# Storing a normalised activation in DRAM with the reloaded three quarters of each channel first

## The chip, the cores and the metric

The kernel runs on one core of a Trainium2 chip. The metric is the device time of one execution in microseconds (us), lower is better. The kernel before takes 1568.49 us (median; 1566.84 to 1569.18).

The engines are called PE (matmul), PEld (its weight loads), DVE (vector), ACT (activations), POOL (GpSimd) and SP or SyncE. SyncE computes nothing here; it issues DMAs. A "q" after an engine's name in the profile (SPq) means its instruction queue. L32 is the line of a helper through which most operations are recorded, so tiles, not lines, tell the operations apart. To "issue" a DMA is to start it by an instruction; it "lands" when its data has arrived, which it tells on a semaphore, a counter that other instructions can wait for. A packet is what a DMA engine moves at a time, in these traces one contiguous run.

## The reference, cut to what matters

An image of 512 x 512 pixels and 96 channels goes through a depthwise 3x3 convolution, a layer norm over the channels, a 96-to-384 matmul with gelu, a global response norm, a 384-to-96 matmul, and a residual add.

```python
h = _layernorm(out, axis=-1)                  # out: the depthwise convolution
h = jnp.einsum('bhwc,ce->bhwe', h, w1)        # C = 96 -> 4C = 384
h = _gelu(h)
gx = jnp.sqrt((h * h).sum(axis=(1, 2), keepdims=True) + 1e-6)   # over the whole image
nx = gx / (gx.mean(axis=-1, keepdims=True) + 1e-6)
h = grn_gamma * (h * nx) + grn_beta + h
h = jnp.einsum('bhwe,ec->bhwc', h, w2)
return x + h
```

The norm `gx` needs a sum over the whole image before any output can be made. So the kernel has two phases: phase 1 computes the gelus once and sums their squares, phase 2 makes the output. The gelus of the whole image are 201 MB (262,144 pixels x 384 x 2 B); the kernel keeps a quarter of them in DRAM and computes the rest a second time.

## The kernel before

The image is cut into 128 blocks of 4 rows (`GR = 4`, `W = 512`). `yn` is the layer norm's result for a block. In phase 1 POOL writes `yn` to SBUF with the row and a third of the channels on the partitions, and SyncE turns it into channels on partitions by way of DRAM: four writes, one for each row, then one read. One quarter of each row's gelus (the "kept" quarter) is also stored in DRAM. Phase 2 reloads `yn`, expands the other three quarters again, and loads the kept one. The last two blocks (`is_res`) stay on chip.

```python
def yn_rows(q):                       # phase 2's load: three quarters of each row
    k = kept_quads(q) * 128           # 128, or 256 for the last two blocks
    return yn_dram[q:q + 2].rearrange("q c (r w) -> (q c) r w", r=GR)[0:128, :, k:]

def yn_dst(q, r):                     # phase 1's write of row r
    return yn_dram[q].rearrange("(c i) (r w) -> r c i w", i=NI, r=GR)[r]
# ...
def stage_write(b):
    yn = yns.pop(b)                   # [128 = 4 rows x 32, NI = 3, W = 512]
    for r in range(GR):
        sp.dma_start(out=yn_dst(b, r), in_=yn[32 * r:32 * r + 32, :, :])

def stage_read(b):
    t = yn_ring[b % NYT]
    sp.dma_start(out=t[:C], in_=yn_src(b))
```

In a slot of phase 1 SyncE's instructions stand in this order; it works them off one by one, and waits in that order too:

```python
load_x(s + 4)                         # input, 432 KB
stage_read(...)                       # yn back: waits until that block's writes have landed
stage_write(...)                      # four writes
stage_bcast(...); stage_rows(...)     # 4 and 2 small DMAs, each once in four blocks
store()                               # kept gelus (g_dram), 384 KB, waits for ACT
```

Phase 2, two parts:

```python
(pq if q % 3 == 0 else sq).dma_start(                # kept gelus: every third load from POOL
    out=kept[:].rearrange("p t j w -> p (t j w)"), in_=g_dram[q])
# ...
LEAD = RES * UPB + 2                                 # 8 gelu units ahead at the start
even = LEAD + (n * NSUB + sub + 1) * (total + 2 - LEAD) / (NSUB * NBLK)   # 2 at the end
```

Of the kernel before, what the change touches and what calls it, by code (L numbers as in the profile page):

```python
# [12 lines left out]
GR = 4  # L13
# [40 lines left out]
def kernel(  # L54
# [13 lines left out]
    bf16 = x.dtype  # L68
    assert bf16 == mybir.dt.bfloat16

    B, H, W, C = x.shape
# [3 lines left out]
    NI = C // 32  # L75
# [6 lines left out]
    NQ = GR * W // QW  # L82
    dram = ctx.enter_context(tc.tile_pool(name="dram", bufs=1, space=bass.MemoryType.DRAM))
    g_dram = dram.tile([NBLK, 128, NCH * QW], bf16, name="g_dram")
    yn_dram = dram.tile([NBLK, C, GR * W], bf16, name="yn_dram")
    r_dram = dram.tile([NBLK, GR, W], bf16, name="r_dram")

    def is_res(q):
        return q >= NBLK - RES

    def cm_quads(q):
        return 3 if q % 3 and not is_res(q) else 2

    def kept_quads(q):
        return 2 if is_res(q) else 1
# [4 lines left out]
    PXP = GR * W // 128  # L100
    MB = W // PXP

    def quad(flat_ap, t):
        return flat_ap.rearrange("p r (t g m) -> p t g r m", t=NQ, m=MB)[:, t]

    def quad_out(flat_ap):
        return flat_ap.rearrange("p (g r m) -> p g r m", r=GR, m=MB)

    def yn_src(q):
        return yn_dram[q].rearrange("c (r w) -> c r w", r=GR)  # L110

    def yn_rows(q):
        k = kept_quads(q) * 128
        return yn_dram[q:q + 2].rearrange("q c (r w) -> (q c) r w", r=GR)[0:128, :, k:]

    def yn_dst(q, r):
        return yn_dram[q].rearrange("(c i) (r w) -> r c i w", i=NI, r=GR)[r]

    consts = ctx.enter_context(tc.tile_pool(name="consts", bufs=1))
    prepool = ctx.enter_context(tc.tile_pool(name="pre", bufs=1))  # L120
# [8 lines left out]
    w1p = consts.tile([128, E], bf16, name="w1p")  # L129
# [14 lines left out]
    grp = {}  # L144
    res_g = {q: prepool.tile([128, 2, NCH, QW], bf16, name=f"resg{q}") for q in range(NBLK - RES, NBLK)}
    NYT = 6
    yn_ring = [prepool.tile([128, GR, W], bf16, name=f"ynT{i}") for i in range(NYT)]

    ynts = {}

# [9 lines left out]
    with ExitStack() as p1:  # L160
        pe, dve, act, pool, sp = (InOrder(tc, e) for e in (nc.tensor, nc.vector, nc.scalar, nc.gpsimd, nc.sync))
# [32 lines left out]
        zrow = consts.tile([128, W], bf16, name="zrow")  # L194
# [15 lines left out]
        make_identity(nc, ident_f[:])  # L210
        pool.memset(Wq[:], 0.0)
        for t in yn_ring:
            pool.dma_start(out=t[C:128, :, :], in_=zrow[C:128, None, :].to_broadcast([128 - C, GR, W]))
        dve.tensor_copy(out=ident_b[:], in_=ident_f[:])
        for q in range(GR):
            dve.tensor_copy(out=eye32[32 * q:32 * q + 32, :], in_=ident_f[32 * q:32 * q + 32, 32 * q:32 * q + 32])
# [12 lines left out]
        for i in range(NXT):  # L229
            t = xtpool.tile([128, NI, SL * MB], bf16, name=f"xT{i}")  # L230
# [6 lines left out]
        def stage_load(n, sq, pq):  # L237
            q = ORDER[n]
            v = (ORDER[0] + n) % NYT
            r0 = q * GR  # L240
            if is_res(q):
                kept, ynt = res_g[q], ynts[q]
            else:
                kept = late.gl.tile([128, 1, NCH, QW], bf16, name="gl")
                (pq if q % 3 == 0 else sq).dma_start(  # L245
                    out=kept[:].rearrange("p t j w -> p (t j w)"), in_=g_dram[q])
                ynt = yn_ring[v]
                sq.dma_start(out=ynt[:, :, kept_quads(q) * 128:], in_=yn_rows(q))
            xr = late.xr.tile([128, PXP, C], bf16, name="xr")
            pq.dma_start(out=xr[:], in_=x[0, r0:r0 + GR].rearrange("r w c -> (r w) c").rearrange(  # L250
                "(p g) c -> p g c", g=PXP))
            grp[q] = dict(kept=kept, ynt=ynt, xr=xr)

        def recompute_units(q):
            nk = kept_quads(q)
            ynt = grp[q]["ynt"]

            def fresh(j):
                if j == 0:
                    grp[q]["made"] = late.gr.tile([128, NCH, (NQ - 1) * QW], bf16, name="gr")  # L260
                if is_res(q):
                    U = psU.tile([128, 2, QW], f32, name="U")
                else:
                    U = late.psU2.tile([128, NQ - 1, QW], f32, name="U2")
                for t in range(nk, NQ):
                    pe.matmul(quad_out(U[:, t - nk, :]), lhsT=w1p[:, j * 128:(j + 1) * 128],
                               rhs=quad(ynt[:], t), start=True, stop=True)
                n = (NQ - nk) * QW
                act.activation(out=grp[q]["made"][:, j, :n], in_=U[:].rearrange("p k w -> p (k w)")[:, :n],
                                func=ACTF.Gelu_apprx_tanh)  # L270

            return [lambda j=j: fresh(j) for j in range(NCH)]
# [73 lines left out]
        for i in range(NI):  # L346
            dve.tensor_copy(out=dwx[:, i], in_=dw9[:, None, chans(i)].to_broadcast([9, GR, 32]))
            pe.matmul(Ud[:, i, :], lhsT=dwx[:, i].rearrange("p q c -> p (q c)"), rhs=ident_b[:9, :9],
                      start=True, stop=True)
# [3 lines left out]
        n = 0  # L353
        for h in range(2):
            for j in range(GR):
                for q in (2 * h, 2 * h + 1):
                    a = q + GR * shift(h, j) - j + 1
                    if 0 <= a < 3:
                        n += 1
                        (dve if n % 2 else pool).tensor_copy(out=Wq[32 * q:32 * q + 32, :, :, j, :],  # L360
                                        in_=Wd[32 * q:32 * q + 32, :, 3 * a:3 * a + 3, :])
# [227 lines left out]
        def stage_write(b):  # L589
            yn = yns.pop(b)  # L590
            for r in range(GR):
                sp.dma_start(out=yn_dst(b, r), in_=yn[32 * r:32 * r + 32, :, :])

        def stage_read(b):
            t = yn_ring[b % NYT]
            sp.dma_start(out=t[:C], in_=yn_src(b))
            ynts[b] = t

        bsts = {}
# [8 lines left out]
        def px0(b):  # L608
            return NCH * QW * (cm_quads(b) - 2)

        def mlp_units(b):
            gsh = res_g[b] if is_res(b) else gshpool.tile([128, 2, NCH, QW], bf16, name="gsh")
            gms[b] = gmpool.tile([128, TAIL], bf16, name="gm")
            yt = ynts[b]

            def cm_mm(dst, j, t):
                pe.matmul(quad_out(dst), lhsT=w1p[:, j * 128:(j + 1) * 128], rhs=quad(yt[:], t), start=True, stop=True)

            def pair(j):
                U = psU.tile([128, 2, QW], f32, name="U")  # L620
                for t in range(2):
                    cm_mm(U[:, t, :], j, t)
                act.activation(out=gsh[:, :, j, :], in_=U[:], func=ACTF.Gelu_apprx_tanh)

            def rest(n):
                U = psU.tile([128, 2, QW], f32, name="U")
                Uf = U[:].rearrange("p k w -> p (k w)")
                c0 = 2 * QW * n
                c, end = c0, c0 + 2 * QW
                while c < end:  # L630
                    if c < px0(b):
                        j, sz = c // QW, QW
                        cm_mm(Uf[:, c - c0:c - c0 + sz], j, 2)
                    else:
                        k, e0 = divmod(c - px0(b), E)
                        sz = min(E - e0, 512 - c % 512, end - c)
                        t, r = divmod(k, GR)
                        col = (cm_quads(b) + t) * 128
                        pe.matmul(Uf[:, c - c0:c - c0 + sz], lhsT=yt[:, r, col:col + 128], rhs=w1p[:, e0:e0 + sz],
                                  start=True, stop=True)  # L640
                    c += sz
                act.activation(out=gms[b][:, c0:end], in_=Uf, func=ACTF.Gelu_apprx_tanh)

            def entry(j, m, src):
                k, e = divmod(ents[b] + m, 32)
                if k not in bsts:
                    bsts[k] = bstpool.tile([128, NCH, 32, 6], f32, name="bst")
                dve.bn_stats(out=bsts[k][:, j, e, :], in_=src)

            def squares(j):  # L650
                for m in range(2):
                    entry(j, m, gsh[:, m, j, :])

            def squares_rest():
                if px0(b):
                    for j in range(NCH):
                        entry(j, 2, gms[b][:, j * QW:(j + 1) * QW])

            def store():
                sp.dma_start(out=g_dram[b], in_=gsh[:, 0].rearrange("p j w -> p (j w)"))  # L660

            return pair, rest, squares, squares_rest, store

        def gram_mms(b):
# [22 lines left out]
        for k, (b0, n) in enumerate(BATCHES):  # L687
# [16 lines left out]
            for b in range(b0, b0 + n):  # L704
# [4 lines left out]
                m = s + (3 if ramp else 4)  # L709
# [11 lines left out]
        for s in range(last_slot + 1):  # L721
# [3 lines left out]
            for b in get("read"):  # L725
                stage_read(b)
            for b in get("write"):
                stage_write(b)
# [49 lines left out]
            else:  # L778
                b = mlp[0]
# [51 lines left out]
            for n in {2: (0, 1, 2), 1: (3, 4)}.get(last_slot - s, ()):  # L831
                stage_load(n, sp, pool)
# [14 lines left out]
    with p2:  # L847
# [14 lines left out]
        r = gi[:].bitcast(f32)  # L862
        for it in range(3):
# [5 lines left out]
            r = rn_[:]  # L869
# [28 lines left out]
        for n, q in enumerate(ORDER):  # L898
            if n + PRE < NBLK:
                stage_load(n + PRE, nc.sync, nc.gpsimd)  # L900
            if n + 2 < NBLK:
                stage_xb(ORDER[n + 2], nc.gpsimd, B2c)
            if n == NBLK - 1:
                stage_out(*held)
                held = None
            o_sb = stage_mm2(n, q)
            if held:
                stage_out(*held)
            held = (q, o_sb)
# [30 lines left out]
```

## Time and profile before

| stretch | length | what fills it |
|---|---|---|
| phase 1, to the first gelu of phase 2 | 1021.0 us | PE and ACT 94% in the middle; SyncE 71% (below) |
| phase 2, from there to the end | 542.2 us | ACT 99%, PE 99%, POOL 94%, DMA share 1.03 (1120 to 1500 us) |

The windows view gives each engine's busy us in a stretch, with the number of instructions, then the granted PE clock, the mean busy share of the 16 DMA engines (packet times summed over 16 engines' time, so it can read a little over 1), and GB/s. The kernel before, the middle of phase 1 and most of phase 2:

```profile
core 0: us, PE busy (x) PEld busy (x) DVE busy (x) ACT busy (x) POOL busy (x), PEclk, DMA share, GB/s
...
400.00:700.00 300.00, 281.96 (x5117) 141.58 (x5114) 257.12 (x438) 281.12 (x280) 267.19 (x201) 1.00 0.77 237
```

```profile
1120.00:1500.00 380.00, 376.52 (x5304) 274.24 (x5303) 201.22 (x374) 375.85 (x277) 356.79 (x218) 1.00 1.03 387
```

No column shows SyncE: issuing a DMA is not counted as busy. It has to be read from the timeline of its queue. Two blocks of the kernel before (start in us, duration in us, instruction, how many merged):

```profile
607.30 0.33 SPq L32 DMA_DIRECT2D ynT<-yn_dram  x1
607.68 2.56 SPq L32 DMA_DIRECT2D yn_dram<-yn  x4
610.28 2.21 SPq L32 DMA_DIRECT2D rbc<-r_dram  x4
612.61 0.55 SPq L32 DMA_DIRECT2D g_dram<-gsh  x1
613.26 0.37 SPq L32 DMA_DIRECT2D xin<-in_x_dram  x1
614.39 0.33 SPq L32 DMA_DIRECT2D ynT<-yn_dram  x1
614.76 2.53 SPq L32 DMA_DIRECT2D yn_dram<-yn  x4
618.00 0.33 SPq L32 DMA_DIRECT2D g_dram<-gsh  x1
618.75 0.34 SPq L32 DMA_DIRECT2D xin<-in_x_dram  x1
622.61 0.33 SPq L32 DMA_DIRECT2D ynT<-yn_dram  x1
```

The four writes of `yn` are the largest item: about 0.6 us each. They are issue times alone; the semaphore records show that such a write lands 4.5 us after its issue (median, 400 to 700 us). The Trainium skill, "Perfetto Trace Analysis", DMA Instruction — HWDGE, says the same of the recorded window: it runs from the semaphores being satisfied until the sequencer is free, and the data movement is not in it. Gaps such as 614.39 less 613.63 (when the load of x was issued) are waits. Who ended them, in the same 300 us (total us, times, longest):

```profile
SPq L32 <- DMA yn_dram<-yn: 42.0, 32, 4.7
SPq L32 <- POOL yn L32: 18.2, 10, 4.0
SPq L32 <- DVE rt L32: 10.8, 7, 1.9
SPq L32 <- DVE xT L32: 8.0, 12, 2.5
```

In this text, SyncE's *occupied* time is the sum of the durations of its instructions plus the step from one to the next (about 45 ns; up to 55 ns of each gap is counted so); the rest of its gaps is *wait*. Over 100 blocks (block 20 to 120, from the start of one block's first gelu to the next one's) the kernel before takes 7.41 us a block, of which SyncE is occupied 5.29 us (issues 4.73, steps 0.57) and waits 2.11 us.

### The profile page before, as it was taken

To read this page: it belongs to the slowest core of one execution; us is meant where nothing else is said; L and a number is where in the kernel's file an instruction comes from. 1 tells how busy PE (TensorE), PEld (TensorE's weight loads), DVE (VectorE), ACT (ScalarE), POOL (GpSimd) and SP (SyncE) were. 2 spreads that over 40 slices of the span, in tenths; PEclk is the share of its full clock that TensorE was granted. 3 is DMA by queue.
4 is the path that set the end of the run, shared out by engine and by line. 5 is a ranking of instruction groups with operands and counts; after the bars stand their busy time and mean duration, and the time that the engine had idled before them with its cause. 6 is when DMAs were issued, how large, how long until landed. Compare 5 with 4: busy or idle time off the path is not lost. (4 is left out here: it accounts for less than half of the span.)

```text
span 1563.2 us, 55720 instructions
## 1 busy us (share of the span) xinstructions
PE 1450.2 (93%) x23749; PEld 844.8 (54%) x23749; DVE 1129.5 (72%) x2027; ACT 1447.1 (93%) x1306; POOL 1314.2 (84%) x933
## 2 busy tenths in 40 slices
PE   7888999999999999999999997789999999999997
PEld 3444444444444444444444444457777777777765
DVE  6748978888898888889888888855555555555544
ACT  3889989999999999999999999989999999999997
POOL 3559888998989898998889897459999999999994
PEclk9999999999999999999999999999999999999999
DMA  5668787787778677777778667869999999999993
GB/s 148 182 182 269 224 262 217 240 254 227 225 234 259 210 249 244 230 235 237 247 210 243 213 197 230 268 238 387 393 379 396 387 397 388 383 381 388 379 372 147
DMA packets 235470, 427.94 MB, mean 274 GB/s; under 512 B 34102, under 2 KB 148374, under 8 KB 235222
## 3 DMA queue, kind: packets, MB, share of 16 engines
q1 hardware_dynamic: 219972, 356.59, 70.2%
q0 software_dynamic: 13888, 67.64, 11.4%
q8 instruction: 186, 3.05, 0.8%
q14 instruction: 62, 0.51, 0.1%
q10 hardware_dynamic: 1362, 0.15, 0.1%
HBM read 272.78 MB, written 150.72 MB: 271 GB/s over the span
## 5 line engine op out<-in xcount | busy, mean ns | idle before, releaser
L32 PE MATMUL U<-ynT,w1p 128*128 128x512 bf16 x2166 | 603.1, 380 | 43.5 <-ACT gm L32 8.7
L32 DVE BATCH_NORM_STATS2 bst<-gsh 128x6 f32<-128x512 bf16 x756 | 468.7, 673 | 128.9 <-ACT gsh L32 128.4
L32 ACT ACTIVATE gr<-U 128x1536 bf16<-128x1536 f32 (+1 forms) x384 | 521.0, 1450 | 17.3 <-PE U L32 14.6
L32 POOL TENSOR_TENSOR yn<-y_bf,rbc 128x1536 bf16<-128x1536 bf16 x128 | 396.9, 3103 | 81.0 <-ACT rbc L32 29.7
L32 DVE TENSOR_TENSOR o_sb<-O,xb 128x384 bf16<-128x384 f32 x512 | 277.5, 557 | 252.2 <-PE O L32 179.7
L278 POOL TENSOR_TENSOR xb<-xr,B2c 128x1536 f32<-128x1536 bf16 x126 | 394.9, 3134 | 43.4 <-DVE B2c L32 35.2
L32 ACT ACTIVATE gsh<-U 128x1024 bf16<-128x1024 f32 x378 | 369.4, 1024 | 55.8 <-ACT gm L32 29.6
L32 ACT ACTIVATE gm<-U 128x1024 bf16<-128x1024 f32 x384 | 368.1, 1035 | 0.6 <-PE U L32 0.5
L32 PE MATMUL Y<-xT,Wq 64*32 64x511 bf16 (+1 forms) x8694 | 320.9, 388 | 9.8 <-DVE B2bc_f L32 3.7
L32 POOL TENSOR_TENSOR ysq<-y_bf 128x1536 bf16<-128x1536 bf16 x114 | 313.2, 2748 | 14.0 <-ACT y_bf L32 13.4
L32 PEld LDWEIGHTS <-w1p 128*128 128x128 bf16 x2166 | 169.4, 97 | 277.9 <-issue 174.2
L32 PEld LDWEIGHTS <-gr 128*128 128x128 bf16 x4584 | 228.7, 98 | 84.4 <-ACT gr L32 12.1
L32 PE MATMUL O<-W2s,gr 128*128 128x96 bf16 x4584 | 251.3, 206 | 12.1 <-ACT gr L32 9.4
L32 PEld LDWEIGHTS <-Wq 64*32 64x32 bf16 x9216 | 102.2, 90 | 187.5 <-issue 146.9
L32 PE MATMUL U<-w1p,ynT 128*128 128x384 bf16 (+2 forms) x1032 | 161.3, 272 | 33.7 <-ACT gm L32 30.6
L32 ACT ACTIVATE y_bf<-Y 128x1536 bf16<-128x1536 f32 x121 | 175.1, 1447 | 16.6 <-PE Y L32 16.4
L32 DVE STREAM_TRANSPOSE xT<-xin 128x576 f32<-128x576 f32 (+1 forms) x256 | 181.2, 747 | 3.2 <-DMA xin<-in_x_dram 3.1
L32 DVE BATCH_NORM_STATS2 bst<-gm 128x6 f32<-128x512 bf16 x252 | 156.5, 676 | 0.9 <-ACT gm L32 0.9
L32 PEld LDWEIGHTS <-ynT 128*128 128x128 bf16 x1032 | 88.7, 96 | 90.8 <-issue 69.4
L32 PE MATMUL SG<-gm 128*128 128x128 bf16 x2064 | 136.3, 219 | 0.5 <-ACT gm L32 0.3
L32 PEld LDWEIGHTS <-gm 128*128 128x128 bf16 x2064 | 121.0, 98 | 11.5 <-issue 0.5
L250 POOL DMA_DIRECT2D xr<-in_x_dram x123 | 67.6, 549 | 27.6 <-POOL xb L278 27.6
(103 smaller groups left out, 700.3 us busy)
## 6 DMA issues: line engine op xcount, KB each, us to landing
ynT<-yn_dram SPq DMA_DIRECT2D x254, 384.0 KB
xin<-in_x_dram SPq DMA_DIRECT2D x126, 432.0 KB
yn_dram<-yn SPq DMA_DIRECT2D x512, 96.0 KB
xr<-in_x_dram POOLq DMA_DIRECT2D x128, 384.0 KB, 6.6
out_dram<-o_sb SPq DMA_DIRECT2D x127, 384.0 KB
g_dram<-gsh SPq DMA_DIRECT2D x126, 384.0 KB
gl<-g_dram SPq DMA_DIRECT2D x84, 384.0 KB
gl<-g_dram POOLq DMA_DIRECT2D x42, 384.0 KB, 6.4
```

The costliest lines, as they stand in the source:

```text
L32: r = f(*a, **k)
L250: pq.dma_start(out=xr[:], in_=x[0, r0:r0 + GR].rearrange("r w c -> (r w) c").rearrange("(p g) c -> p g c", g=PXP))
L278: pq.tensor_tensor(out=xb[:], in0=grp[q]["xr"][:], in1=bias[:, None, :].to_broadcast([128, PXP, C]), op=ALU.add)
```

## The change

Intent: phase 2 loads the three quarters it expands as four runs of 768 B for each channel. If those quarters lie together in DRAM, it is one run of 3 KB, a quarter of the packets. The SBUF tile gets the same order. For this, each row's write in phase 1 has to be split in two, for the two regions. Core of the diff:

```diff
     def yn_rows(q):
+        n = GR * (NQ - kept_quads(q)) * 128
+        return yn_dram[q:q + 2].rearrange("q c w -> (q c) w")[0:128, :n]
+
+    def yn_dst(q, r):
         k = kept_quads(q) * 128
-        return yn_dram[q:q + 2].rearrange("q c (r w) -> (q c) r w", r=GR)[0:128, :, k:]
-
-    def yn_dst(q, r):
-        return yn_dram[q].rearrange("(c i) (r w) -> r c i w", i=NI, r=GR)[r]
+        n = GR * (W - k)
+        dst = yn_dram[q].rearrange("(c i) w -> c i w", i=NI)
+        return [(slice(k, W), dst[:, :, r * (W - k):(r + 1) * (W - k)]),
+                (slice(0, k), dst[:, :, n + r * k:n + (r + 1) * k])]
 ...
             for r in range(GR):
-                sp.dma_start(out=yn_dst(b, r), in_=yn[32 * r:32 * r + 32, :, :])
+                for cols, dst in yn_dst(b, r):
+                    sp.dma_start(out=dst, in_=yn[32 * r:32 * r + 32, :, cols])
 ...
-                sq.dma_start(out=ynt[:, :, kept_quads(q) * 128:], in_=yn_rows(q))
+                src = yn_rows(q)
+                sq.dma_start(out=ynt[:, :src.shape[1]], in_=src)
```

The rest of the diff (cut) reads the matmul operands from their new places in the tile.

More of the change, by code (lines that the diff above doesn't have):

```diff
@@ L101, with quad, pixel_cols @@
     MB = W // PXP
-    def quad(flat_ap, t):
-        return flat_ap.rearrange("p r (t g m) -> p t g r m", t=NQ, m=MB)[:, t]
+    def quad(yt, b, t):
+        k = kept_quads(b)
+        n = GR * (NQ - k) * 128
+        part, t, m = (yt[:, n:], t, k) if t < k else (yt[:, :n], t - k, NQ - k)
+        return part.rearrange("p (r t g m) -> p t g r m", r=GR, t=m, m=MB)[:, t]
+    def pixel_cols(b, r, t):
+        k = kept_quads(b)
+        return (r * (NQ - k) + t - k) * 128
     def quad_out(flat_ap):
         return flat_ap.rearrange("p (g r m) -> p g r m", r=GR, m=MB)
-    def yn_src(q):
-        return yn_dram[q].rearrange("c (r w) -> c r w", r=GR)
     def yn_rows(q):
+        n = GR * (NQ - kept_quads(q)) * 128
+        return yn_dram[q:q + 2].rearrange("q c w -> (q c) w")[0:128, :n]
+    def yn_dst(q, r):
         k = kept_quads(q) * 128
-        return yn_dram[q:q + 2].rearrange("q c (r w) -> (q c) r w", r=GR)[0:128, :, k:]
-    def yn_dst(q, r):
-        return yn_dram[q].rearrange("(c i) (r w) -> r c i w", i=NI, r=GR)[r]
+        n = GR * (W - k)
+        dst = yn_dram[q].rearrange("(c i) w -> c i w", i=NI)
+        return [(slice(k, W), dst[:, :, r * (W - k):(r + 1) * (W - k)]),
+                (slice(0, k), dst[:, :, n + r * k:n + (r + 1) * k])]
     consts = ctx.enter_context(tc.tile_pool(name="consts", bufs=1))
@@ L146 @@
     NYT = 6
-    yn_ring = [prepool.tile([128, GR, W], bf16, name=f"ynT{i}") for i in range(NYT)]
+    yn_ring = [prepool.tile([128, GR * W], bf16, name=f"ynT{i}") for i in range(NYT)]
     ynts = {}
@@ L212 @@
         for t in yn_ring:
-            pool.dma_start(out=t[C:128, :, :], in_=zrow[C:128, None, :].to_broadcast([128 - C, GR, W]))
+            pool.dma_start(out=t[C:128, :].rearrange("p (r w) -> p r w", w=W),
+                           in_=zrow[C:128, None, :].to_broadcast([128 - C, GR, W]))
         dve.tensor_copy(out=ident_b[:], in_=ident_f[:])
@@ L266, in fresh @@
                     pe.matmul(quad_out(U[:, t - nk, :]), lhsT=w1p[:, j * 128:(j + 1) * 128],
-                               rhs=quad(ynt[:], t), start=True, stop=True)
+                               rhs=quad(ynt[:], q, t), start=True, stop=True)
                 n = (NQ - nk) * QW
@@ L591, in stage_write @@
             for r in range(GR):
-                sp.dma_start(out=yn_dst(b, r), in_=yn[32 * r:32 * r + 32, :, :])
+                for cols, dst in yn_dst(b, r):
+                    sp.dma_start(out=dst, in_=yn[32 * r:32 * r + 32, :, cols])
         def stage_read(b):
             t = yn_ring[b % NYT]
-            sp.dma_start(out=t[:C], in_=yn_src(b))
+            sp.dma_start(out=t[:C], in_=yn_dram[b])
             ynts[b] = t
@@ L616, in cm_mm @@
             def cm_mm(dst, j, t):
-                pe.matmul(quad_out(dst), lhsT=w1p[:, j * 128:(j + 1) * 128], rhs=quad(yt[:], t), start=True, stop=True)
+                pe.matmul(quad_out(dst), lhsT=w1p[:, j * 128:(j + 1) * 128], rhs=quad(yt[:], b, t), start=True, stop=True)
             def pair(j):
@@ L637, in rest @@
                         t, r = divmod(k, GR)
-                        col = (cm_quads(b) + t) * 128
-                        pe.matmul(Uf[:, c - c0:c - c0 + sz], lhsT=yt[:, r, col:col + 128], rhs=w1p[:, e0:e0 + sz],
+                        col = pixel_cols(b, r, cm_quads(b) + t)
+                        pe.matmul(Uf[:, c - c0:c - c0 + sz], lhsT=yt[:, col:col + 128], rhs=w1p[:, e0:e0 + sz],
                                   start=True, stop=True)
```

## The prediction

> **What bounds it now.** The page's slices show two stages. Phase 1 (about 0 to 1020 us) makes yn, writes it to DRAM, reads it back and runs the first MLP; phase 2 (to 1563 us) reloads it.
> - Phase 2, windows view, 1120 to 1200 us: ACT busy 79.89 of 80, PE 80.00, POOL 74.85, DMA share 1.03 at 388 GB/s. ACT's gelus over 128x1536 start 1.33 us apart when back to back; three a block are 4.0 us, and blocks do start 4.02 to 4.07 us apart. DMA is about as full (1.57 MB a block at 390 GB/s is 4.0 us), but the waits view lists no PE or ACT wait for a DMA there. The last 20 blocks take 4.4 to 5.5 us because PE and ACT wait for each other. So ACT binds.
> - Phase 1, window 400 to 700 us: 40 blocks, 7.5 us each; PE 281.96 and ACT 281.12 of 300; DMA share 0.77. SyncE, which no busy row shows, issues everything here: 339 DMAs whose issues sum to 192 us, plus some 45 ns between them. About 85 us are left, 2.1 us a block, of which about 1 us is the wait for yn writes to land before the read (SyncE's waits: 117.7 us over 100 to 1000).
>
> **What the change does.**
> - Phase 2 reads: 512 packets of 768 B (37 ns each) become 128 of 3 KB (124 ns): 18.9 to 15.9 us, 0.19 us over 16 engines, 5% of a block's DMA. The issue falls from 0.52 to about 0.33 us. ACT stays at 4.0 us, so I expect 0 to 8 us in all.
> - Phase 1 reads stay at 4 KB a channel; matmul operands keep 32-element runs. No change.
> - Phase 1 writes: 4 DMAs a block become 8 (32 partitions x 3 runs, of 768 B or 256 B). Packet time barely moves: 384 x 55 ns before; 384 x 37 plus 384 x about 18 after (estimate between 64 B at 11 ns and 768 B). The Trainium skill, "DMA: Bandwidth & Descriptors", Specifications, puts 512 B as the least for line rate, with read-modify-write below; this trace has no 256 B packet, so it could cost more. The issue cost is the main thing: a yn write takes 0.60 us of SyncE plus 0.045. Four more are 2.6 us a block against 2.1 us of slack.
>
> **On the critical path.** SyncE comes onto it in phase 1. A block's sum: issues 4.5 us, gaps 0.5, the four new ones 2.6, landing wait (a yn write lands 2.2 us after issue at best, 4.5 at the median) 0.3 to 0.8: about 7.6 to 8.2 us against 7.5. I take 7.9: +0.4 us on about 122 blocks, +49 us, less about 4 us in phase 2.
>
> **Predicted: 1612 us, 8 in 10 between 1575 and 1670.** Faster by over 2%: 0.04; within 2%: 0.27; slower by over 2%: 0.69.
>
> **What would show it.** Phase 1 ends 15 to 100 us later; in the 400 to 700 window fewer than 40 blocks, PE and ACT under 280 of 300; 8 yn writes a block at 0.6 us, SyncE waiting less for POOL's yn. Phase 2's block period unchanged at 4.0 us, its DMA share about 0.98.
>
> **What would make it wrong.** Shorter issues for the new writes (0.33 us as flat ones take) would hide them: within 1%. Costly 256 B packets would push it over 1670. If phase 2 was really DMA-paced, it would gain some 20 us and the sum would stay within 2%.

## The result, and the profile after

The changed kernel takes 1730.88 us (median of 4; 1727.54 to 1735.03). The ratio to the kernel before is 1.104 (95% interval 1.101 to 1.107). The direction was predicted; the loss, 162 us, is over three times the predicted 44, and lies outside the range.

The first gelu of phase 2 starts at 1191.3 us instead of 1021.0, and from there to the end it is 540.8 us instead of 542.2. So phase 1 lost 170 us between these two profiles and phase 2 took 1.4 us less. That difference is not due to the new layout: e1, e3 and e9 below, which keep the old loads, took 540.8 to 540.9 us there too. The windows view of the changed kernel, the same stretch of phase 1 and a stretch of phase 2:

```profile
400.00:700.00 300.00, 252.36 (x4345) 127.13 (x4341) 220.40 (x374) 242.97 (x240) 227.80 (x176) 0.95 0.69 201
```

```profile
1300.00:1500.00 200.00, 199.25 (x2819) 145.69 (x2816) 107.43 (x199) 198.93 (x147) 187.77 (x114) 1.00 1.01 389
```

In phase 1 every column fell: PE from 282 to 252 us, ACT from 281 to 243, the DMA engines from 0.77 to 0.69. Nothing in that table is the bottleneck, which points to what it does not list. In phase 2 ACT and PE are as full as before, and only the DMA share moved, from 1.03 to 1.01. SyncE's queue in the changed kernel:

```profile
437.04 0.38 SPq L32 DMA_DIRECT2D xin<-in_x_dram  x1
437.52 0.41 SPq L32 DMA_DIRECT2D ynT<-yn_dram  x1
437.98 5.77 SPq L32 DMA_DIRECT2D yn_dram<-yn  x8
443.84 0.53 SPq L32 DMA_DIRECT2D g_dram<-gsh  x1
444.47 0.38 SPq L32 DMA_DIRECT2D xin<-in_x_dram  x1
445.11 0.32 SPq L32 DMA_DIRECT2D ynT<-yn_dram  x1
445.48 6.30 SPq L32 DMA_DIRECT2D yn_dram<-yn  x8
451.88 0.54 SPq L32 DMA_DIRECT2D g_dram<-gsh  x1
```

and what it waited for from 400 to 700 us, the longest first:

```profile
SPq L32 <- DMA xin<-in_x_dram: 7.0, 11, 1.3
SPq L32 <- DVE bst L32: 5.8, 12, 1.3
SPq L32 <- DMA ynT<-yn_dram: 5.1, 16, 0.9
SPq L32 <- DMA yn_dram<-yn: 4.8, 10, 1.6
```

The large waits for POOL's `yn` and for the landing of the writes are gone: SyncE is late for everything now. Over blocks 20 to 120 a block takes 8.72 us, of which SyncE is occupied 8.24 (95%) and waits 0.48. The 1.31 us more a block, on about 125 blocks, are 164 us: about the whole loss.

### The profile page after: what moved, and what is told of

Read it like the earlier page. It is cut to its first block, busy times and chain, and to the rows that moved or that the text cites. A ratio compares the mean times of both kernels' runs of the same rounds, so it can differ in the third digit from the quotient of the medians.

```text
span 1732.1 us, 56379 instructions
## 1 busy us (share of the span) xinstructions
PE 1510.1 (87%) x23749; PEld 873.5 (50%) x23749; DVE 1130.7 (65%) x2027; ACT 1455.8 (84%) x1306; POOL 1313.2 (76%) x933
## 5 line engine op out<-in xcount | busy, mean ns | idle before, releaser
L32 PE MATMUL U<-ynT,w1p 128*128 128x512 bf16 x2166 | 612.0, 385 | 80.9 <-ACT gsh L32 41.0
L32 ACT ACTIVATE gm<-U 128x1024 bf16<-128x1024 f32 x384 | 377.0, 1033 | 93.8 <-PE U L32 92.2
L32 PE MATMUL Y<-xT,Wq 64*32 64x511 bf16 (+1 forms) x8694 | 334.2, 403 | 11.7 <-DVE B2bc_f L32 3.7
L32 PEld LDWEIGHTS <-gr 128*128 128x128 bf16 x4584 | 228.7, 98 | 84.4 <-ACT gr L32 12.1
L32 PE MATMUL O<-W2s,gr 128*128 128x96 bf16 x4584 | 251.3, 206 | 12.1 <-ACT gr L32 9.4
L32 PE MATMUL U<-w1p,ynT 128*128 128x384 bf16 (+2 forms) x1032 | 179.4, 295 | 22.1 <-ACT gm L32 18.9
L32 PE MATMUL SG<-gm 128*128 128x128 bf16 x2064 | 153.2, 233 | 0.7 <-DVE SG L32 0.4
L32 PEld LDWEIGHTS <-gm 128*128 128x128 bf16 x2064 | 136.8, 106 | 13.8 <-issue 4.2
L32 PEld LDWEIGHTS <-ynT 128*128 128x128 bf16 x1032 | 94.6, 104 | 80.9 <-issue 59.0
L32 PE MATMUL SG<-rowsel,ysq 128*128 128x4 bf16 x1536 | 57.6, 167 | 82.6 <-POOL ysq L32 82.5
```

The lines of the kernel that those rows point to most:

```text
L32: r = f(*a, **k)
```

## The experiments

The theory, S: SyncE's own time for issuing binds phase 1, since a write of `yn` costs it about 0.6 us whatever it moves. The rivals are P, the new packets of 256 B and 768 B; L, the new layout as the matmuls and loads see it; and N, the number of DMAs in flight with the semaphores they need. "Block" is us a block over blocks 20 to 120, "occupied" and "wait" are SyncE's, as defined above; phase 2 runs from its first gelu to the end. Before and changed kernel stand for comparison.

| run | yn writes a block | time, us | ratio to before | block | occupied | wait | phase 2, us |
|---|---|---|---|---|---|---|---|
| before | 4 | 1568.5 | 1 | 7.41 | 5.29 | 2.11 | 542.2 |
| changed | 8 | 1730.9 | 1.104 | 8.72 | 8.24 | 0.48 | 540.8 |
| e1_split_channels | 8 | 1745.7 | 1.113 | 8.80 | 8.15 | 0.65 | 540.9 |
| e2_new_reads_only | 4 | 1566.9 | 0.999 | 7.42 | 5.43 | 1.98 | 540.8 |
| e3_split_columns | 8 | 1726.0 | 1.102 | 8.60 | 8.18 | 0.42 | 540.8 |
| e4_kept_in_one | 5 | 1576.4 | 1.005 | 7.41 | 6.48 | 0.93 | 540.8 |
| e5_six_writes | 6 | 1602.8 | 1.023 | 7.68 | 6.86 | 0.81 | 541.3 |
| e8_seven_writes | 7 | 1664.6 | 1.062 | 8.07 | 7.42 | 0.65 | 541.2 |
| e6_flat_one_write | 1 | 1583.2 | 1.011 | 7.41 | 3.03 | 4.38 | 561.5 |
| e7_flat_eight_writes | 8 | 1661.5 | 1.063 | 7.94 | 6.55 | 1.40 | 554.4 |
| e9_drains_on_syncE | 4 | 1787.3 | 1.140 | 9.17 | 8.94 | 0.22 | 540.8 |
| e10_constant_lead | 4 | 1563.0 | 0.998 | 7.41 | 5.37 | 2.03 | 540.2 |
| e11_pool_relieved | 4 | 1551.1 | 0.989 | 7.41 | 5.44 | 1.97 | 524.2 |
| e12_kept_in_one_pool_relieved | 5 | 1558.8 | 0.994 | 7.41 | 6.49 | 0.92 | 524.4 |

All results were correct except e2.

### e1: the count of writes alone, in the old layout

```diff
-                sp.dma_start(out=yn_dst(b, r), in_=yn[32 * r:32 * r + 32, :, :])
+                for c in (0, 16):
+                    sp.dma_start(out=yn_dst(b, r)[c:c + 16], in_=yn[32 * r + c:32 * r + c + 16, :, :])
```

> The kernel before, its layout unchanged, with each of the four yn writes of a block cut into two of 16 partitions: 8 writes a block, but the same bytes in the same 384 packets of 1 KB. Theory S (SyncE's issue time binds phase 1; a write costs it about 0.64 us whatever it moves): 1700 to 1740 us, about 8.6 to 8.8 us a block in phase 1, SyncE without idle time. Rival P (the 256 B packets and their slower landing): no small packets here, so 1568 us within 1%. Rival L (the new SBUF layout slows the matmuls or the read): the old layout is kept, so 1568 us within 1%.

1745.7 us, just over the expected range. Eight writes of half the partitions, with the same packets of 1 KB as the kernel before, cost as much as the change and a little more. Their issue takes 0.65 us on average against 0.62 in the kernel before, though each moves half. So neither P nor L is needed for a loss of this size; e2 to e4 test whether they add to it.

### e2: everything of the new layout but the count of writes

```diff
 # in the changed kernel; pixels are permuted, the result is wrong on purpose
-                for cols, dst in yn_dst(b, r):
-                    sp.dma_start(out=dst, in_=yn[32 * r:32 * r + 32, :, cols])
+                sp.dma_start(out=dst[r], in_=yn[32 * r:32 * r + 32, :, :])   # old 1 KB runs
```

> The changed kernel with the old four writes of 1 KB runs a block, so pixels are permuted and the result is wrong on purpose; all of the new layout's reads, 3 KB loads and matmul strides stay. Theory S: 1560 to 1570 us, phase 1 as before at 7.5 us a block, phase 2 as in both kernels at 4.0 us a block, since ACT paces it. Rival P: the same, 1560 to 1570. Rival L: still about 1730 us.

1566.9 us, ratio 0.999 (0.997 to 1.001). With four writes the new layout costs nothing. Its phase 2, with the 3 KB loads, takes 540.8 us, as in e1, e3 and e9 with the old ones: the loads by themselves are worth nothing that shows here. The 542.2 us of the profile before lie in two of its first blocks (4.46 and 5.33 us, against 3.82 and 4.60 in e2, and the same in e10 with the old loads).

### e3: the columns split as in the change, old layout

```diff
-                sp.dma_start(out=yn_dst(b, r), in_=yn[32 * r:32 * r + 32, :, :])
+                for cols in (slice(k, W), slice(0, k)):
+                    sp.dma_start(out=yn_dst(b, r)[:, :, cols], in_=yn[32 * r:32 * r + 32, :, cols])
```

> The kernel before, its layout unchanged, with each yn write cut by columns as the change cuts it: 8 writes a block, packets of 768 B and 256 B as in the change, old reads. Theory S and rival P: about 1730 us (S: within 1% of the split by channels; P: this one alone is slow). Rival L: 1568 us.

1726.0 us, with the change's packet sizes. It is 1% faster than e1, which has no small packets at all, so the packets of 256 B add nothing that can be seen here. In the changed kernel such a packet took 18 ns and one of 768 B 36 ns (medians).

### e4: the change with five writes

```diff
+            # three quarters: one write for each row, as in the change; kept quarter:
+            dst = yn_dram[b, :, GR * (W - k):].rearrange("(c i) (r w) -> r c i w", i=NI, r=GR)
+            sp.dma_start(out=dst, in_=yn[:, :, :k])
```

> The changed kernel, same layout and same 768 B and 256 B packets, with the kept quarter of all four rows written by one DMA: 5 writes a block instead of 8. Result correct. Theory S: SyncE has 2.1 us a block of slack in the kernel before and one more write takes 0.65, so 1565 to 1580 us, 7.5 us a block. Rival P: the packets are the same, so about 1730 us still. Rival L: about 1730 us.

1576.4 us, and correct: the change nearly free of its cost, with the same packets. The block is back at 7.41 us. The remaining 0.5% lies outside blocks 20 to 120: its phase 2 starts at 1033.9 us, against 1020.7 to 1027.1 in the profiles of runs with at most four writes (e9 aside). The trace puts it at the end of phase 1: from the first gelu of block 120 to that of block 127 it takes 49.8 us, and the kernel before 40.4. In that stretch one issue of the store of kept gelus took 6.31 us; why was not looked into.

### e5 and e8: six and seven writes

The edit of e1 on two rows of four, and on three.

> The kernel before with two of its four writes a block cut in two by channels: 6 writes, packets unchanged. Theory S as a sum: the changed kernel's SyncE fills 8.82 us a block with 8 writes; a write is 0.64 us plus 0.045, so 6 writes make 7.45 us, level with the 7.5 us that PE and ACT need: 1568 to 1600 us, the knee. A rival in which each added write costs the same (delay handed straight on, a quarter of the loss each): 1655 us.

> As the last with three of the four writes cut: 7 writes. Theory S as a sum: 8.14 us a block, 0.64 more than 7.5 on about 126 blocks: 1640 to 1665 us. The rival in which each added write costs the same: about 1700 us.

1602.8 (a little over the expected range) and 1664.6 us, against 1567 with four and 1746 with eight. The first two added writes cost 18 us each, the seventh 62, the eighth 81. So there is slack that is used up first; the rival of a constant cost a write falls. The knee is soft: at six writes SyncE is occupied 6.86 us, still below the 7.41 that the other engines need, and the block already takes 7.68. A queue that works in order and must wait for others now and then can lose before it is full. But N may have a part in it too. In e5 the longest item among SyncE's waits (400 to 700 us) is the landing of the load of x, which in the kernel before made up 3.7 us:

```profile
SPq L32 <- DMA xin<-in_x_dram: 16.2, 15, 2.4
```

In all 15 cases the DMA that waits is the eighth after that load on SyncE's queue and uses the same semaphore, which is N as e7 below shows it. No run parts the two at six writes.

### e6 and e7: the same number of DMAs with a cheaper issue

`yn` is kept in DRAM as it lies in SBUF, so that a write is a plain run of 3 KB for each partition, in one DMA (e6) or in eight of 16 partitions (e7). The reads then gather.

```diff
-    yn_dram = dram.tile([NBLK, C, GR * W], bf16, name="yn_dram")
+    yn_dram = dram.tile([NBLK, 128, NI * W], bf16, name="yn_dram")
 ...
-        return yn_dram[q].rearrange("c (r w) -> c r w", r=GR)
+        return yn_dram[q].rearrange("(r c) (i w) -> c i r w", r=GR, i=NI)
 ...
+            for p in range(0, 128, 16):             # e7; e6 has one DMA of 128 partitions
+                sp.dma_start(out=yn_dram[b, p:p + 16], in_=yn[p:p + 16].rearrange("p i w -> p (i w)"))
```

> yn kept in DRAM as it lies in SBUF, so that a block is written by one DMA of 128 runs of 3 KB; the reads gather 1 KB runs (phase 1) and 768 B runs (phase 2) and load 96 channels instead of 128. Theory S: SyncE gains some 2 us a block of slack that the kernel before did not lack, phase 2 is paced by ACT: 1555 to 1572 us. If SyncE already cost the kernel before something, it would gain over 1%: under 1552 us.

> The last with the flat write cut into 8 DMAs of 16 partitions: as many DMAs a block as in the changed kernel, each with a plain run of 3 KB a partition, which SyncE issues in about 0.33 us instead of 0.60. Theory S (issue time): 8 x 0.38 = 3.0 us a block against 2.6 in the kernel before, so 1560 to 1580 us. Rival N (the number of DMAs in flight: the kernel has 8 completion semaphores for SyncE's DMAs, so each issue waits for the landing of the one eight before): about 1700 to 1740 us, with SyncE idle in waits for landings.

e6: phase 1 did not gain, although SyncE's occupied time fell to 3.03 us: the block stayed at 7.41 us. So SyncE cost the kernel before nothing in mid phase 1. What e6 lost, against the expected 1555 to 1572 us, is phase 2, 561.5 us. With its gathering loads the DMA engines moved less: from 1250 to 1350 us the windows view shows a share of 1.04 at 354 GB/s, against 389 in the kernel before (362 in e7, which gathers too). Output tiles waited 41.4 us for output to be written, a wait that the kernel before does not have there. (1050 us to the end; us in total, times, longest.) Why its packets are slower was not settled.

```profile
DVE o_sb L32 <- DMA out_dram<-o_sb: 41.4, 24, 5.4
```

e7 fits neither S alone (1560 to 1580) nor N alone (1700 to 1740): 1661.5 us. The flat issues were not as cheap as expected, 0.46 us on average when eight follow each other, so SyncE is occupied 6.55 us. But it also waits 1.40 us a block, and for something new (400 to 700 us):

```profile
SPq L32 <- DMA ynT<-yn_dram: 26.1, 35, 2.0
SPq L32 <- DMA xin<-in_x_dram: 22.6, 20, 2.9
SPq L32 <- DMA yn_dram<-yn: 9.3, 23, 0.7
```

SyncE's DMAs in phase 1 use eight completion semaphores in turn, and one is used again only when its last DMA has landed. With eight writes in a row, the seventh and eighth come eight DMAs after the big load of x and the read of `yn`. One block shows it to the hundredth: the read issued at 402.74 us landed 7.03 us later, at 409.77; the eighth write of that block, on the same semaphore, was issued at 409.79. So N is real and part of the cost of having eight writes. In the changed kernel the same two waits are there, but short (7.0 and 5.1 us in 300), since the writes' longer issue lets the loads land meanwhile: 12.1 us over 34 blocks, 0.36 us a block beside a loss of 1.31.

### e9: SyncE's time alone, no DMA added

```diff
                 sp.dma_start(out=yn_dst(b, r), in_=yn[32 * r:32 * r + 32, :, :])
+                for _ in range(12):
+                    sp.drain()
```

> The kernel before, with no DMA added: after each of its four yn writes SyncE runs 12 empty drain instructions (about 7 ns each in the profile, and 45 ns from one instruction to the next), 48 a block, about 2.5 us of SyncE's time, as much as the four added writes took. Theory S, SyncE's own time alone: SyncE needs 5.5 + 2.5 us a block and some wait, 8.0 to 8.6, so 1630 to 1710 us. Rival N, the number of DMAs and their 8 semaphores alone: 1568 us within 1%. If both matter in the changed kernel, this run lies between before (1568) and the changed kernel (1731), as the split of the flat write did (1661).

1787.3 us, slower than the change, with the four writes of before and no DMA more. The expected number was missed because the delay came out longer than meant: the first drain after each DMA took 0.38 us, so that 48 drains a block filled about 4.0 us (1547 drains between 400 and 700 us, 59.6 us of duration and 45 ns from each to the next), not 2.5. The four writes with what follows them now take over 5 us:

```profile
510.13 0.33 SPq L32 DMA_DIRECT2D g_dram<-gsh  x1
510.56 0.38 SPq L32 DMA_DIRECT2D xin<-in_x_dram  x1
511.16 0.32 SPq L32 DMA_DIRECT2D ynT<-yn_dram  x1
511.57 5.64 SPq L32 DMA_DIRECT2D yn_dram<-yn  x4
```

With the delay as it was, S holds: occupied 8.94 and wait 0.22 of a block of 9.17 us, and no wait for the landing of x or of the read of `yn` in SyncE's list. Time on SyncE's queue, without a single added DMA or packet, slows all of phase 1. S is sufficient; the rival N is not needed for a loss of this size.

The granted PE clock fell along with the pace in every slower kernel (0.952 in the changed kernel's profile, 0.945 here, 0.976 in e7). It fell here with the DMAs of the kernel before, and PE was busy 252 of 300 us in the changed kernel, so I take it for a consequence of PE's idle time. No run held the clock fixed to show it.

### e10, e11, e12: what phase 2 is bound by

The prediction rests on the claim that ACT, not the loads, paces phase 2. e10 tests a part of it, the slow end.

```diff
-            even = LEAD + (n * NSUB + sub + 1) * (total + 2 - LEAD) / (NSUB * NBLK)
+            even = LEAD + (n * NSUB + sub + 1) * UPB / NSUB
```

> The kernel before with one line of phase 2's pacing changed: the gelus made ahead of the second matmul stay 8 units ahead instead of shrinking to 2 by the end. It tests what was said of the end of phase 2. If PE and ACT wait for each other there because the lead is short, the last 20 blocks go at about 4.05 us instead of 4.4 to 5.5 and the run gains 5 to 10 us, with the DMA traffic unchanged: 1556 to 1564 us. If the loads set the pace there, no change: 1568.

1563.0 us, ratio 0.998 (0.996 to 1.001): no gain that is clear of noise. (The profiled execution took 1569.06 us, the slowest of the four by 6 us, and has one block of 8.3 us.) The end no longer slows down, but from about the 45th block on nearly every third block takes 4.5 us instead of 4.03. The gain was given back to another engine. POOL's timeline in e10 shows which:

```profile
1478.48 3.13 POOL L278 TENSOR_TENSOR xb<-xr,B2c 128x1536 f32<-128x1536 bf16 x1
1481.91 0.55 POOL L250 DMA_DIRECT2D xr<-in_x_dram  x1 [0.30 <-POOL xb L278]
1482.49 3.14 POOL L278 TENSOR_TENSOR xb<-xr,B2c 128x1536 f32<-128x1536 bf16 x1
1485.92 0.56 POOL L250 DMA_DIRECT2D xr<-in_x_dram  x1 [0.30 <-POOL xb L278]
1486.47 0.54 POOL L245 DMA_DIRECT2D gl<-g_dram  x1
1487.02 3.14 POOL L278 TENSOR_TENSOR xb<-xr,B2c 128x1536 f32<-128x1536 bf16 x1
```

The second of these blocks starts 4.01 us after the first and the third 4.53 after the second, because POOL issues the load of the kept gelus there. POOL has no free time at all: its add, its issue and the 0.30 us between them fill every block. e11 gives that load to SyncE, which has time in phase 2:

```diff
-                (pq if q % 3 == 0 else sq).dma_start(
+                sq.dma_start(
```

> The constant lead left every third block at 4.5 us: in those POOL issues the load of the kept gelus (0.54 us) besides its own 3.13 us add and the load of x. Here, in the kernel before with the constant lead, SyncE issues all of those loads; it has idle time in phase 2. If POOL's issue was that stop, the 4.5 us blocks go and phase 2 takes 520 to 532 us instead of 542: 1546 to 1560 us. If the DMA engines pace phase 2 once POOL does not (share 1.02 in the kernel before), it stays at 538 or more: 1562 to 1570 us.

1551.1 us, ratio 0.989 (0.987 to 0.990), correct: the fastest kernel. From the fourth block on phase 2 goes at 4.03 us a block to the end. (This load's move without the constant lead was not run.)

```profile
1120.00:1500.00 380.00, 380.00 (x5377) 279.58 (x5375) 210.29 (x377) 380.00 (x284) 345.06 (x189) 1.00 1.04 393
```

ACT is busy 380.00 of 380 us here. POOL is busy 345, but most of the rest is the 0.30 us before each issue: its add, that pause and its issue still make 4.01 us, so it only just fits into 4.03. Does the new layout help where POOL no longer holds a block up? e12 is e11's two edits in e4.

> The same two edits in the new layout with 5 writes a block. Its phase 1 cost about 9 us more than the kernel before. If phase 2 is still paced by engines, its phase 2 is within 2 us of the one with the old layout and the whole is 5 to 12 us slower than it: 1555 to 1570 us. If the DMA engines now pace phase 2, the 3 KB loads (5% fewer engine-us a block) give 8 to 25 us there, and it is the fastest of all: 1535 to 1555 us.

1558.8 us; phase 2 took 524.4 us against 524.2 in e11. The 3 KB loads are worth nothing in phase 2 even there. ACT has no gap: three gelus that start 1.34 us apart are the 4.03 us of a block. PE reads 380.00 of 380 us as well and POOL needs 4.01, so these traces don't show that ACT alone sets the pace; the loads don't. The DMA share reads 1.02 to 1.04 in both, so this number alone would have told the wrong story.

## Why the prediction was right or wrong

- **The mechanism held.** It named the issue cost of four more writes on SyncE in phase 1. e1 (count alone), e2 (all but the count) and e9 (SyncE's time alone) show it. Phase 1's reads, the matmul operands and the packets cost nothing visible (e2, e3), as written.
- **The step that failed is the sum for a block:** "about 7.6 to 8.2 us against 7.5. I take 7.9". Measured: 8.72 against 7.41, so 1.31 us more where 0.4 was forecast. Three things were wrong in it.
  - The addition: its terms as written (4.5, 0.5, 2.6 and 0.3 to 0.8) make 7.9 to 8.4. So 7.9 was their lower end and not the middle.
  - The issues that were there before: put at 4.5 us a block, though the prediction's own 192 us over 40 blocks are 4.8. Measured: 4.73.
  - The four new issues: put at 4 x 0.60 = 2.4 us, the median. The issues of a block rose from 4.73 to 7.50 us, so by 2.77.

  The steps (0.5 + 4 x 0.045 = 0.68, measured 0.74) and the waits (0.3 to 0.8, measured 0.48) were about right. A median misses that issues stretch: between 400 and 700 us, 30 of the changed kernel's 422 took over 0.3 us longer than the median of their kind, and all time above these medians is 32.3 us, 0.95 us a block (20.7 us, 0.52 a block, before). The mean of the trace before, 0.62 us a write, would have given 4.73 + 0.57 + 4 x 0.665 = 7.96, and 8.44 us with the measured waits. The last 0.3 us are issues that became longer in the changed kernel, and their cause stays open. In all, under a third of the loss was predicted.
- **The 2.1 us of "slack" was too simple.** e5 has 1.6 us more occupied SyncE time than before and already loses 0.27 us a block. In-order waits cannot all be filled. And the eight semaphores, which the prediction does not mention, add waits of their own when writes come eight in a row (e7), and some at six (e5).
- **Phase 2 gained nothing that can be shown**, within the 0 to 8 us predicted; the sum took 4. The 1.4 us between the two profiles appear with the old loads too (e1, e3, e9). "So ACT binds" was not the whole reason: in the kernel before POOL had no free time either and the end went slowly, which e10 and e11 uncovered. That does not touch the prediction's sum: with POOL relieved, ACT has no gap and the new loads still gain nothing (e12).
- **The signs named beforehand:** 40 blocks in the 300 us became about 34; PE and ACT fell under 280; eight writes at 0.6 us; SyncE waited less for POOL's `yn`; phase 2's period stayed. All these came out. Two sizes did not: phase 1 ended 170 us later, not 15 to 100, and phase 2's DMA share was 1.01, not about 0.98.
- **What would make it wrong:** costly 256 B packets were named as the way past 1670 us. It went past for another reason; they took the 18 ns estimated.

## What to carry to other kernels

Before splitting a DMA to make a later load more contiguous, add up the issuing queue's time, since the busy table leaves it out, with mean durations rather than medians, and check the addition; here a queue at 71% of the period could take one more 0.6 us write for 0.5%, two for 2% and four for 10%. A DMA share of 1.0 does not show that packets pace a stage: quartering those of a load moved nothing while ACT was full. Slower packets can still cost time, as e6's phase 2 shows (561.5 us). When a gain does not come, look at which engine has no gap left at the place it should have come; here that was POOL, and giving its extra issue to an idle queue, together with a steady lead, took phase 2 from 542 to 524 us.

## What the Trainium skill lacked or had wrong

- "DMA: Bandwidth & Descriptors", Issuing engines are not separate DMA queues, says that the sequencer's time to initiate a DMA "is usually small relative to the DMA itself". Here it decided: a 24 KB write of the kept quarter is 96 packets of 18 ns over 16 engines, 0.11 us of data time (an estimate from these), and its issue took 0.60 us. Against the 3.3 us from issue to landing (median, 400 to 700 us) the issue is the smaller part, as the page has it, but the queue is held by the issue alone.
- "Perfetto Trace Analysis", What "DMA-bound" means, lists this case (a DMA sequencer whose track is solid with DMAs) and names large descriptors as what matters for it. The changed kernel's queue agrees with the first (95% occupied). The remedy fits in part only: e1 has the packets of the kernel before, 1 KB, and is 1.1% slower than e3 with 768 B and 256 B. The number of issues counts. So does their form: one run of 3 KB a partition took 0.30 us to issue after a pause and 0.42 in a row (e7), three runs a partition 0.55 (e9) and 0.60; whether by the length of a run or by their number was not tested. No page I used gives these times by form.
- "Runtime: NRT & Kernel Launch", Instruction fetch mechanics, says that crossing a 16 KiB block of instructions is "mostly hidden". In the changed kernel all 30 issues that took over 0.3 us longer than the median of their kind (400 to 700 us) overlapped one of 35 instruction packets of 16 KB, though only 57 of all 422 issues did; before, it was 18 of 19 with 41 of 339. They overlap; no run here shows that one causes the other.
- "DMA: Bandwidth & Descriptors", Specifications, gives 512 B as the least for line rate, with a read-modify-write below. Packets of 256 B took 18 ns, of 768 B 36 ns: fewer bytes a ns (14 against 21), as the page would have it, but no loss in the run's time (e3 against e1).
- No page I used tells that a SyncE drain right after a DMA issue takes 0.38 us where the ones after it take 7 ns (e9).
